# Seven products instead of eight in the down projections of the last two batches

## The chip, the cores and the metric

The kernel runs on one core of a Trainium2 chip. The metric is device time in microseconds, from launch to the end of the last transfer. TensorE (PE) multiplies, VectorE (DVE), ScalarE (ACT) and GpSimd (POOL) work on elements, SyncE (SP) issues most transfers; ACT issues the stores of the output. Each engine works through its own instructions strictly in order.

## The reference

```python
def _attn_ref(q, k, v):                      # 8 batches, 8 heads, 576 positions, 64 wide
    scores = scale * np.matmul(q, k.transpose(0, 1, 3, 2))
    ...
    mask = (rel >= 0) & (rel < window)       # window = 128
    scores = np.where(mask, scores + bias[None], -1000000000.0)
    ...
    return np.matmul(attn, v).astype(np.float32)

def _moe_ref(x, w_a, w_b, w_out):            # 4608 tokens, 512 -> 1536 -> 512
    a = x @ w_a
    b = x @ w_b
    return (a * b @ w_out).astype(np.float32)
```

Windowed attention feeds a feed-forward layer: two up projections, whose results are multiplied element by element, and one down projection by `w_out`. Inputs and result are float32.

## The kernel before

The work goes batch by batch. For batch b TensorE does the **up** projections (hidden values h, 1536 by 576, as 12 blocks f of 128 rows in two halves t of 288 columns) and then the **down** projection (512 by 576, as 4 blocks e of 128 rows and two halves). Float32 accuracy comes from float16 pairs: every operand is kept as a high and a low half, and one product is three matmuls (high·high, high·low, low·high), each 128 by 128 by 288. Six such matmuls are one *step* of the weave below.

In batches 4 to 7 the up projection already uses the scheme of seven products (`up_fast`, lines 926 to 972): a 2 by 2 block product takes seven block products of sums of blocks, instead of eight. The sums of the weights were made earlier (`sums_of_weights`) and lie in the tile `wsum` and in one quarter of `wup`; those of the inputs are made by `split_x` into `xs`. The steps of two blocks f alternate (two lanes), because each block's sums are read from two PSUM banks while the other lane's steps run. `halve` (line 900) makes the float16 pair of a finished block: one cast on ACT, one subtraction on DVE.

The down projection (`down`, line 998) is plain: for each half t and each e it adds 12 blocks times three matmuls in one PSUM bank, ACT scales the bank to `row` (line 1010) and issues its store (line 1011).

Beside batch b's projections runs the attention of batch b+1, as a generator (`attention`, line 712). It works on pairs of heads, numbered i, four to a batch, and yields seven times per pair. `Pace.along` drives it in step with the projections: it names the place of the generator (in pairs) that is to be reached when n steps are done. For one pair the chain is: loads of q and k, squares and scaling, four layout transfers within the core (lines 385 to 388), the score products (`scores`, line 402; tile `sc_ps`), minimum (DVE) and exponential (ACT), `normalize` (line 427: reciprocals, then the probabilities as float16 pairs in `phl`), a transposing transfer `pT<-phl` issued on SP (line 447), the product with v (`pv`, tile `x_ps`), and `keep_x` (line 452: ACT copies the result, squares it; POOL adds the squares to `xq`, line 472). `phl` and `pT` have one buffer each. When a batch's last pair is done, `split_x` makes the operands of its up projection, and `hidden_scale` (line 552, tile `n_ps`) sums the squares on TensorE.

The order of TensorE's instructions from batch 1 on is the order in which the code is written and woven (`manual_schedule` for PE). The order on the other engines, SP among them, is set by a planner ahead of the run, from a model of the durations; `issue_after` sets a floor for some of them. In the last batches before, the attention goes to place 28 beside batch 6's up projection (84 steps), and from 28 to its end at 29 in the first half of the 48 steps of its down projection.

## Time and profile before

| what | value |
|---|---|
| time, three runs | 975.34 us median, 973.39 to 976.2 |
| span of the profiled execution, first to last instruction | 972.1 us |
| time of the profiled execution itself | not on record; the shortest of the three runs is 1.3 us above the span, the median 3.2 us |
| granted TensorE clock | 0.996 |
| TensorE busy | 958.0 us, 99% of the span |
| busy DVE, ACT, POOL | 681.4, 625.8, 260.1 us |
| batch 6's up projection with its attention | 763.8 to 834.4 us |
| batch 6's down projection | 834.4 to 871.5 us |
| batch 7's up and down projection, no attention beside it | 871.5 to 933.6 and to the end |

The times are of whole runs; the span is of one execution that was profiled, and all places below are microseconds from its first instruction. Matmuls are pipelined: a row of the timeline gives the start of its first and the time to the end of its last; the distance between two starts is what a matmul costs.

### The profile page before, as it was taken

The page shows a single profiled execution, that of the slowest core. Times are in us where ns is not written, and L with a number is a line of the kernel's source. Part 1 is how long each engine was busy: PE and PEld are TensorE (multiplying, and loading weights), DVE is VectorE, ACT ScalarE, POOL GpSimd, SP SyncE. Part 2 cuts the span into 40 slices and gives each one's busy share as a digit, 9 for nine tenths or more (in the row PEclk, how much of TensorE's full clock was granted, in tenths as well). Part 3 has the DMA queues.
Part 4 walks back from the last instruction along what each step waited for, and adds up shares of the span by engine and source line. Part 5 has one row for each costly group of instructions (what it writes and reads, how often), then busy time and mean ns, then how long its engine had stood idle before and what let it go on. Part 6 is the DMA issues. An engine that isn't in the chain of part 4 may idle for free.

```text
span 972.1 us, 23845 instructions
## 1 busy us (share of the span) xinstructions
PE 958.0 (99%) x9340; PEld 748.0 (77%) x9341; DVE 681.4 (70%) x1896; ACT 625.8 (64%) x1701; POOL 260.1 (27%) x307
## 2 busy tenths in 40 slices
PE   8989999999999999999999999999999999999998
PEld 6667777777877777777877777777777778777776
DVE  6999997568888668877677867667666676514520
ACT  6877787577767667776766776767666765423321
POOL 1211132045546033531234222401222122301100
PEclk9999999999999999999999999999999999999999
DMA  9473745626437334454336542464245350210001
GB/s 347 143 275 107 260 90 123 161 81 124 90 85 178 69 69 83 100 156 93 65 79 174 103 100 50 112 177 93 45 94 133 117 98 12 57 37 2 1 13 37
DMA packets 148432, 102.82 MB, mean 106 GB/s; under 512 B 120032, under 2 KB 128352, under 8 KB 147296
## 3 DMA queue, kind: packets, MB, share of 16 engines
q1 hardware_dynamic: 138816, 91.77, 38.7%
q10 hardware_dynamic: 9504, 9.54, 3.0%
q8 instruction: 73, 1.20, 0.5%
q14 instruction: 39, 0.32, 0.1%
HBM read 48.33 MB, written 9.44 MB: 59 GB/s over the span
## 4 chain that ended last, share of the span: by engine, by line
PE 89%; DVE 4%; DMA 3%; ACT 3%; issue 1%; SPq 0%; POOL 0%; ACTq 0%; DVEq 0%; POOLq 0%
PE dn_ps L1005 23%; PE ch L909 19%; PE up_ps L909 18%; PE p L909 15%; PE x_ps L543 5%; PE sc_ps L417 4%; PE dn_ps L871 2%; PE sc_ps L413 1%; DMA v<-in_vP 1%; ACT t L626 0%; DMA qst<-qkl 0%; DVE phl L440 0%; DMA qk<-in_kT 0%; DMA qkl<-qkl 0%; PE tr_ps L632 0%
## 5 line engine op out<-in xcount | busy, mean ns | idle before, releaser
L909 PEld LDWEIGHTS <-wup 128*128 128x128 f16 x3072 | 296.5, 98 | 83.8 <-issue 7.4
L1005 PE MATMUL dn_ps<-h,wdn 128*128 128x288 f16 x2016 | 253.9, 286 | 0.0
L1005 PEld LDWEIGHTS <-wdn 128*128 128x128 f16 x2016 | 193.9, 98 | 51.8
L909 PE MATMUL up_ps<-xs,wup 128*128 128x288 f16 x1536 | 196.4, 287 | 2.1 <-DVE v L672 1.1
L909 PEld LDWEIGHTS <-wsum 128*128 128x128 f16 x1152 | 111.7, 98 | 30.9 <-issue 1.3
L964 POOL TENSOR_TENSOR rc<-rc,row 128x288 f32<-128x288 f32 x64 | 61.8, 965 | 275.3 <-DVE row L962 259.4
L423 ACT ACTIVATE t<-t,mn 128x192 f32<-128x192 f32 (+2 forms) x252 | 107.3, 427 | 25.6 <-DVE mn L422 25.3
L440 DVE SCALAR_TENSOR_TENSOR phl<-t,rin,phl 128x192 f16<-128x192 f32 (+2 forms) x252 | 109.6, 476 | 16.9 <-ACT phl L439 16.6
L909 PE MATMUL p<-xs,wup 128*128 128x288 f16 x768 | 115.1, 286 | 0.0
L909 PE MATMUL ch<-xs,wup 128*128 128x288 f16 x768 | 115.1, 286 | 0.0
L909 PE MATMUL ch<-xs,wsum 128*128 128x288 f16 x768 | 111.5, 286 | 0.4 <-ACT rc L934 0.4
L439 ACT ACTIVATE phl<-t,rin 128x192 f16<-128x192 f32 (+2 forms) x252 | 88.9, 426 | 29.7 <-DVE rin L436 15.9
L901 ACT CAST h<-rc 128x576 f16<-128x576 f32 x96 | 64.1, 668 | 63.5 <-DVE rc L969 37.2
L902 DVE TENSOR_TENSOR h<-rc,h 128x576 f16<-128x576 f32 x90 | 69.3, 770 | 30.1 <-ACT h L901 29.3
L422 DVE CUSTOM_DVE_ANT_0 t<-sc_ps,bias,neg 128x192 f32<-128x192 f32 (+2 forms) x216 | 73.6, 388 | 9.9 <-PE sc_ps L417 9.8
L1010 ACT ACTIVATE row<-dn_ps,oi 128x288 f32<-128x288 f32 x56 | 27.6, 494 | 57.5 <-PE dn_ps L1005 57.5
L478 DVE TENSOR_TENSOR xs<-v,xs 128x576 f16<-128x576 f32 x52 | 48.0, 934 | 22.6 <-ACT xs L477 22.5
L946 ACT ACTIVATE row<-ch,g 128x288 f32<-128x288 f32 x64 | 31.8, 497 | 48.9 <-PE ch L909 48.8
L941 DVE TENSOR_TENSOR rc<-p,rc 128x288 f32<-128x288 f32 x64 | 29.0, 454 | 44.6 <-PE p L909 33.8
L398 POOL TENSOR_SCALAR bias<-rel_sb,ninv,sl_sb 128x192 f32<-128x192 f32 x24 | 23.6, 983 | 137.1 <-DVE mn L422 119.1
L909 PE MATMUL p<-xs,wsum 128*128 128x288 f16 x384 | 57.6, 286 | 0.0
L969 DVE SCALAR_TENSOR_TENSOR rc<-rc,g,ch 128x288 f32<-128x288 f32 x64 | 32.6, 510 | 23.6 <-PE ch L909 23.4
(158 smaller groups left out, 1375.8 us busy)
## 6 DMA issues: line engine op xcount, KB each, us to landing
v<-in_vP SPq DMA_DIRECT2D x8, 1280.0 KB, 6.2
out<-row ACTq DMA_DIRECT2D x62, 144.0 KB, 1.9
qk<-in_qT SPq DMA_DIRECT2D x28, 288.0 KB, 4.0
qk<-in_kT SPq DMA_DIRECT2D x28, 288.0 KB, 4.4
wdn<-in_w_a SPq DMA_DIRECT2D x12, 512.0 KB, 5.1
wdn<-in_w_b SPq DMA_DIRECT2D x12, 512.0 KB, 6.1
wdn<-in_w_out SPq DMA_DIRECT2D x12, 512.0 KB, 4.6
qst<-qkh SPq DMA_DIRECT2D x24, 144.0 KB, 2.8
```

What stands on the lines that cost most here:

```text
L417: pe.matmul(ps[64 * e:64 * e + 64, c:c + w], o.qs[:, e, qq], ks[:, e, kk], start=not last, stop=last)
L422: beside[1] = vec.tensor_tensor_reduce(out=t[:, c:c + w], in0=ps[:, c:c + w], in1=o.bias[:, WIN - w:WIN], scale=-0.125 if o.b == 1 else o. ...
L423: beside[0] = act.activation(t[:, c:c + w], t[:, c:c + w], AF.Exp, bias=o.mn[:, n:n + 1], scale=-1.0, accum_out=o.sm[:, n:n + 1])
L439: beside[0] = last_phl[0] = act.activation(phl[:, 0, pc:pc + w], e, AF.Copy, scale=s)
L440: beside[1] = vec.scalar_tensor_tensor(out=phl[:, 1, pc:pc + w], in0=e, scalar=s, in1=phl[:, 0, pc:pc + w], op0=ALU.mult, op1=ALU.subtract)
L478: vec.tensor_tensor(out=xs[:, n, 1, :, :], in0=src, in1=xs[:, n, 0, :, :], op=ALU.subtract)
L543: last = pe.matmul(xp[oc // 512][64 * h:64 * h + 64, o0:o0 + w], vt[0:rows, c:c + 64], probs(pt, rows, blocks, h), start=(n == 0 and first ...
L901: act.copy(h[:, f, :, 0, :], hid)
L902: eng.tensor_tensor(out=h[:, f, :, 1, :], in0=hid, in1=h[:, f, :, 0, :], op=ALU.subtract)
L909: pe.matmul(ps[:, 0:HT], w[:, wi, k, :], xs[:, b, xi, k, :], start=(first and n == 0), stop=(last and n == len(ks) - 1), skip_group_check= ...
L964: pool.tensor_tensor(out=x0, in0=x0, in1=mid, op=ALU.mult)
L1005: pe.matmul(ps[:, 0:HT], wdn[:, f, wi, e * P:(e + 1) * P], h[:, f, t, hi, :], start=(m == 0 and n == 0), stop=(m == NF - 1 and n == 2))
```

## The change

Batches 6 and 7 (`b >= SEVEN`) do their down projection by seven products as well (`down_fast`). The blocks of `w_out`, of the hidden values and of the output are taken as 2 by 2: two blocks f (2j, 2j+1), two halves t, and the output's row blocks e in two groups g, with e and e+2 together. Each group's seven products run over six pairs j with three matmuls: 18 matmuls to a product, 126 to a group, 252 to a batch, where `down` has 288. The two groups alternate product by product.

What this needs:

- Sums of hidden blocks. In these two batches `up_fast` collects two blocks f in a `quad`, `halve_quad` makes four differences per pair on POOL and seven halves instead of four (four casts on ACT, four subtractions on DVE), at set numbers of steps after the pair's last product. Three of the seven have their place in `hx`, in the part of `wup` that belongs to blocks 6 to 11.
- Sums of `w_out` (`sums_of_down`), made once, beside batches 4 and 5: for each of 12 pieces five POOL instructions, a cast, a subtraction, and a transfer of 256 KB to DRAM (`kept_dn`). Three quarters are loaded beside batch 6's up projection into `wdx`, in the part of `wsum` of blocks 6 to 11 (12 transfers of 192 KB); one quarter goes into `wdn` ahead of it (4 transfers).
- Batch 6 works through blocks 6 to 11 first, since their weights are overwritten. Batch 7 needs them again: `keep_up` copies their seven forms to DRAM beforehand (42 transfers of 128 KB), and batch 7's first six blocks load each form into the place of the form just used.
- The attention goes to place 27.2 instead of 28 beside batch 6's up projection. Beside its down projection (42 steps instead of 48) it is paced to reach 30 in 34 steps, so it ends (29) about step 22.

```diff
@@ setup @@
-    xs = const.tile([P, 8, 2, 2, HT], F16, name="xs")
+    xr = const.tile([P, 8 * 4 * HT + 3 * 4 * HT], F16, name="xr")
+    xs = xr[:, 0:8 * 4 * HT].rearrange("p (n w k t) -> p n w k t", n=8, w=2, k=2)
+    hids = cycle([xr[:, (8 + n) * 4 * HT:(9 + n) * 4 * HT]... for n in range(3)])
+    quads = cycle([xr[:, (7 + 2 * n) * 4 * HT:(9 + 2 * n) * 4 * HT]... for n in range(2)])
...
+    def keep_up():
+        for f in range(NF // 2, NF):
+            for n in range(7):
+                sp.dma_start(kept_up[f - NF // 2, :, 4 * P * n:4 * P * n + 4 * P], form_of(f, n))
+                yield
+    def sums_of_down():
...
+            pool.tensor_tensor(out=a[:, 0, :], in0=a[:, 3, :], in1=a[:, 0, :], op=ALU.subtract)
+            pool.tensor_tensor(out=a[:, 2, :], in0=a[:, 2, :], in1=a[:, 0, :], op=ALU.subtract)
+            yield
+            both = work.tile([P, 512], F32, tag="t", name="ws16", bufs=4)...
+            with tc.issue_after(last_main[0].ins):
+                act.copy(both[:, :, 0, :], a)
+            vec.tensor_tensor(out=both[:, :, 1, :], in0=a, in1=both[:, :, 0, :], op=ALU.subtract)
+            sp.dma_start(kept_dn[n], both.rearrange("p a w q -> p (a w q)"))
+            yield
+    def load_down_sums():
+        for n in range(NF):
+            sp.dma_start(wdx[:, n].rearrange("p a w q -> p (a w q)"), kept_dn[n, :, 0:6 * P])
+            yield
...
@@ hidden_scale @@
-            ps = bank("n_ps") if states else ps_at.tile([P, 512], F32, tag="at", name="n_ps")
+            ps = ps_ef.tile([P, 512], F32, tag="ef", name="n_ps") if started["down"] >= SEVEN else bank("n_ps") if states else ...
@@ up_fast @@
+    def halve_slots(h, j, n, x):
+        out = halves_of(h, j, n)
+        act.copy(out[:, :, 0, :], x)
+        vec.tensor_tensor(out=out[:, :, 1, :], in0=x, in1=out[:, :, 0, :], op=ALU.subtract)
+    def difference(out, a, b):
+        pool.tensor_tensor(out=out, in0=a, in1=b, op=ALU.subtract)
+    def halve_quad(h, f, quad, last):
+        j = f // 2
+        b11, b12, b22, b21 = (quad[:, n, :] for n in range(4))
+        if f % 2 == 0:
+            after(1 if last else 2, lambda: halve_slots(h, j, 6, quad[:, 0:1, :]))
+            after(2 if last else 5, lambda: difference(b11, b12, b11))
+            return
+        for n, k, fn in (
+            (2, 1, lambda: halve_slots(h, j, 0, quad[:, 2:4, :])),
+            (3, 1, lambda: difference(b12, b22, b12)),
+            (5, 2, lambda: difference(b22, b22, b11)),
+            (6, 4, lambda: halve_slots(h, j, 2, quad[:, 0:2, :])),
+            (7, 3, lambda: difference(b21, b21, b22)),
+            (10, 5, lambda: halve_slots(h, j, 4, quad[:, 2:4, :])),
+        ):
+            after(k if last else n, fn)
...
+        def load(n):
+            if first_half:
+                sp.dma_start(form_of(where[f], n), kept_up[f, :, 4 * P * n:4 * P * n + 4 * P])
...
         terms(ch, (f, 0), 0, True, True)
+        load(0)
...
+    def down_fast(b, oi, h, pairs):
+        started["down"] = b
...
+        slots = (6, 1, 0, 5, 2, 4, 3)
+        def product(ps, g, q, x, first, last):
+            n = 0
+            for j in pairs:
+                hid = slot_of(h, j, slots[x])
+                for wi, hi in ((0, 0), (0, 1), (1, 0)):
+                    pe.matmul(ps, weight(q, j, wi, g), hid[:, hi, :], start=(first and n == 0), stop=(last and n == 17), skip_group_check=True)
+                    n += 1
+                    if n % 6 == 0 and n < 18:
+                        yield
...
+        def group(g):
+            ch = ps_ch.tile([P, 512], F32, tag="ch", name="dch")[:, 0:HT]
...
+            yield from product(ch, g, 0, 0, True, True)
+            with tc.high_priority(offset=PRIO):
+                last_read[0] = last_main[0] = act.activation(x0, ch, AF.Copy, scale=oi)
+                first_reads[:] = first_reads[1:] + last_read
+            yield
+            ps = ps_ef.tile([P, 512], F32, tag="ef", name="d2")[:, 0:HT]
+            yield from product(ps, g, 1, 1, True, True)
+            with tc.high_priority(offset=PRIO):
+                last_dve[0] = vec.scalar_tensor_tensor(out=x0, in0=ps, scalar=oi, in1=x0, op0=ALU.mult, op1=ALU.add)
+            store(x0, g, 0)
+            yield
...
+        lanes = [group(0), group(1)]
+        for _ in range(7):
+            for lane in lanes:
+                for _ in range(3):
+                    next(lane)
+                    tick()
+                    yield
@@ batch @@
-        weave(att.along(up(states[b], h, plain, fast), n, NPAIR * b + 4), *((spread, *x) for x in quota[b][0]))
-        weave(att.along(down(b, out_scale(states[b]), h, plain + fast), 48, NPAIR * b + 6), *((spread, *x) for x in quota[b][1]))
...
+        for n, z in ((0, 84), (1, 48)):
+            if SEVEN - 2 <= b < SEVEN:
+                sides[n] += [(spread_down, 0, z, 9), (keeping, 0, z, 11)]
+        if b == SEVEN:
+            sides[0] += [(loading, 52, 84, NF)]
+            load_first_sums()
+        weave(att.along(up(states[b], h, plain, fast, seven, b > SEVEN), n_up, NPAIR * b + (3.2 if b == SEVEN else 4)), *sides[0])
+        if seven:
+            weave(att.along(down_fast(b, out_scale(states[b]), h, [f // 2 for f in fast[::2]]), 34, NPAIR * b + 6))
+        else:
+            weave(att.along(down(b, out_scale(states[b]), h, plain + fast), 48, NPAIR * b + 6), *sides[1])
```

How the instructions stand now, at two places. First ACT, around the end of batch 6's up projection: before, from the second half of the last pair's exponentials (line 423) to the last of its probabilities (line 439); the rows between are the up projection's own (PSUM reads of lines 934, 946 and 952, casts of line 901).

```order
L423 ACTIVATE t_12776,sm_12309<-t_12776,mn_12308 128x192 x2
L946 ACTIVATE row_12704<-ch_12702,g_11613 128x288
L952 COPY rc_12703<-p7_12819 128x288
L901 CAST h_774<-rc_12661 128x2x288
L934 COPY rc_12852<-ch_12851 128x288
L901 CAST h_774<-rc_12703 128x2x288
L946 ACTIVATE row_12853<-ch_12851,g_11613 128x288
L435 ACTIVATE rin_12310<-sm_12309 128x4
L952 COPY rc_12852<-p7_12895 128x288
L934 COPY rc_12904<-ch_12903 128x288
L439 ACTIVATE phl_130<-t_12713,rin_12310 128x192 x2
L439 ACTIVATE phl_130<-t_12776,rin_12310 128x192 x2
```

And in the changed kernel, from the first PSUM read of the down projection (line 1180) to the copy of the last pair's product with v (line 504, `keep_x`):

```order
L1180 ACTIVATE row_13017<-dch_13016,oi_13012 128x288
L991 CAST h_778<-xr_125 128x2x288
L471 ACTIVATE t_13108,sm_12533<-t_13108,mn_12532 128x192
L991 CAST wup_120<-xr_125 128x2x288
L1180 ACTIVATE row_13131<-dch_13130,oi_13012 128x288
L483 ACTIVATE rin_12534<-sm_12533 128x4
L487 ACTIVATE phl_134<-t_13045,rin_12534 128x192 x2
L487 ACTIVATE phl_134<-t_13108,rin_12534 128x192 x2
L1172 DMA out_0<-row_13017 128x288
L1172 DMA out_0<-row_13131 128x288
L1191 ACTIVATE xr_125<-dch_13016,oi_13012 128x288
L504 ACTIVATE v_11747<-x_ps_13229 128x512
```

The same piece of attention (old lines 423, 435, 439 are new lines 471, 483, 487) has moved from the up projection into the down projection: its last exponential stands behind the first PSUM read of `down_fast`, its probabilities behind the second. On TensorE 78 matmuls now lie between the pair's last score product and its product with v; before there were 138 of the up projection and 66 of the down projection.

Second SP, at the load of v for batch 5 (during batch 3's down projection); the four layout transfers follow it, for the pair whose scores open batch 4's up projection. Before:

```order
L447 DMA_TRANSPOSE pT<-phl 128x32x128
L297 DMA v<-in_vP 128x2560
L385 DMA qst<-qkh 64x1152
L386 DMA qst<-qkl 64x1152
L345 DMA qk<-in_qT 64x2x576
L387 DMA qkh<-qkh 64x1152
L388 DMA qkl<-qkl 64x1152
```

Now:

```order
L495 DMA_TRANSPOSE pT<-phl 128x32x128
L345 DMA v<-in_vP 128x2560
L296 DMA kept_up<-wup 128x512
L296 DMA kept_up<-wsum 128x512 x3
L433 DMA qst<-qkh 64x1152
L434 DMA qst<-qkl 64x1152
L393 DMA qk<-in_qT 64x2x576
L435 DMA qkh<-qkh 64x1152
L436 DMA qkl<-qkl 64x1152
```

Four copies to DRAM have come between v and the layout transfers. The planner has done the same at the load of v for batch 4; at those for batches 6 and 7 one copy of `kept_dn` stands there.

133 lines of the change are left out of this document (119 added, 14 removed).

## The prediction

> **What bounds the kernel now.** I read the page's busy shares first, then the waits of TensorE, then its timeline around batch 6.
>
> ```profile
> PE 958.0 (99%) x9340; PEld 748.0 (77%) x9341; DVE 681.4 (70%) x1896; ACT 625.8 (64%) x1701; POOL 260.1 (27%) x307
> PE sc_ps L417 <- DMA qkh<-qkh: 1.2, 1, 1.2
> PE sc_ps L417 <- DMA qkl<-qkl: 0.4, 1, 0.4
> 834.42 8.25 PE L1005 MATMUL dn_ps<-h,wdn 128*128 128x288 f16 x66
> 842.59 1.54 PE L543 MATMUL x_ps<-pT,vhl 128*64 128x128 f16 x42
> 844.06 7.52 PE L1005 MATMUL dn_ps<-h,wdn 128*128 128x288 f16 x60
> 851.42 0.41 PE L558 MATMUL n_ps<-xq,ones 128*128 128x512 bf16 x2
> 851.67 20.01 PE L1005 MATMUL dn_ps<-h,wdn 128*128 128x288 f16 x162
> 871.51 0.90 PE L909 MATMUL ch<-xs,wup 128*128 128x288 f16 x6
> ```
>
> TensorE is the bound. In the waits of its engine over the last 430 us I find one place alone, 1.6 us for layout transfers. So a matmul taken away shows in full, as long as no wait takes its place. One costs (871.51 - 851.67) / 162 = 0.1225 us.
>
> **The change part by part. Matmuls.** `down` has 2 x 4 x 12 x 3 = 288 to a batch, `down_fast` 2 x 7 x 6 x 3 = 252, on the same shape (128x288 float16). 72 fewer in two batches, 72 x 0.1225 = **-8.8 us**. The up projections and the attention keep theirs.
>
> **The last pair's product with v.** This is what I expect to give half of it back. The scores of pair 27 (banks 2 and 3) now stand two steps into batch 6's down projection, and only 78 matmuls, 78 x 0.1225 = 9.6 us, lie between them and `x_ps`. In that time the exponentials, `normalize` and the transposing transfer must be through. The rows of the same piece before (ACT, then DVE, SP and the answer on line 447), where the matmul behind the last score started at 817.46:
>
> ```profile
> 817.46 0.91 PE L909 MATMUL p<-xs,wup 128*128 128x288 f16 x6
> 818.55 0.44 ACT L423 ACTIVATE t<-t,mn 128x192 f32<-128x192 f32 x1
> 818.99 0.44 ACT L423 ACTIVATE t<-t,mn 128x192 f32<-128x192 f32 x1
> 827.33 0.20 ACT L435 ACTIVATE rin<-sm 128x4 f32<-128x4 f32 x1
> 828.31 1.49 ACT L439 ACTIVATE phl<-t,rin 128x192 f16<-128x192 f32 x4
> 830.16 0.73 DVE L440 SCALAR_TENSOR_TENSOR phl<-t,rin,phl 128x192 f16<-128x192 f32 x2
> 830.97 4.84 SPq L447 DMA_TRANSPOSE pT<-phl  x1
> DMA to landing us min/median/max: 6.7/7.1/9.2
> ```
>
> Before, the transfer was issued at 830.97, landed some 7 us later, and the product began at 842.59: 4.5 us to spare. Now I count from the matmul behind the last score. The first exponential starts at 818.55 - 817.46 = 1.1 as before. ACT then has, by its order, a PSUM read, a cast, the second exponential, a cast and the second PSUM read ahead of `rin`. For their distances:
>
> ```profile
> 845.19 0.68 ACT L471 ACTIVATE sq<-v 128x576 bf16<-128x576 f32 x1
> 845.78 0.66 ACT L477 CAST xs<-v 128x576 f16<-128x576 f32 x1
> 846.34 0.49 ACT L1010 ACTIVATE row<-dn_ps,oi 128x288 f32<-128x288 f32 x1
> 846.73 0.66 ACT L477 CAST xs<-v 128x576 f16<-128x576 f32 x1
> ```
>
> A cast of 576 columns costs 0.56, a PSUM read 0.39, an exponential 0.44 (818.99 - 818.55). So `rin` starts at 1.1 + 2 x 0.44 + 2 x 0.39 + 2 x 0.56 = 3.9 us; the second PSUM read's matmuls end at 24 x 0.1225 = 2.9 and don't hold it. From `rin` to the last low half of `phl` it took 830.16 + 0.73 - 827.33 = 3.6 us, with two foreign DVE instructions between; now one. I take 2.9, so `phl` is complete at 6.8 and `pT` lands at 6.8 + 7.1 = 13.9. TensorE stands from 9.6 to 13.9: **+4.3 us**. The bounds: `phl` at 6.2 with the shortest landing (6.7) gives 3.3; `phl` at 7.5 with the longest (9.2) gives 7.1. Nothing else in TensorE's order is allowed past `x_ps`, so the whole wait counts. What lies before it (the product with v of pair 26) has its `pT` from far earlier.
>
> **The sums of squares behind it.** `n_ps` needs ACT's copy and square and POOL's addition:
>
> ```profile
> 843.98 0.71 ACT L456 ACTIVATE v<-x_ps 128x512 f32<-128x512 f32 x2 [4.46 <-PE x_ps L543]
> 846.21 1.79 POOL L472 TENSOR_TENSOR xq<-xq,sq 128x576 bf16<-128x576 bf16 x1
> ```
>
> That ends at 848.00, 3.9 us after the last product with v (844.06). Before, 60 matmuls (7.4 us) covered it; now 30 do, 30 x 0.1225 = 3.7 us. The order on ACT and POOL there is the same: **+0.3 us**, bounds 0 and 1.0. After that 132 matmuls (16.2 us) remain until batch 7's first step, so its operands and scale are no issue.
>
> **Transfers on SP's queue.** The 42 copies of up weights and 12 of down sums run beside batches whose TensorE never waits for loads, except at one kind of place: the first scores of batches 3 to 6's up projection, behind v and the layout transfers. Batch 3's and batch 4's, first DMA, then SP and PE:
>
> ```profile
> DMA  9999992667999989995733841799989999787400
> v<-in_vP SPq DMA_DIRECT2D x1, 1280.0 KB, 6.6
> qkl<-qkl SPq DMA_DIRECT2D x1, 144.0 KB, 3.7
> 414.98 0.54 SPq L297 DMA_DIRECT2D v<-in_vP  x1
> 423.53 0.46 SPq L388 DMA_DIRECT2D qkl<-qkl  x1
> 427.79 0.22 PE L417 MATMUL sc_ps<-qkh,qst 128*64 128x64 f16 x2
> 526.80 0.54 SPq L297 DMA_DIRECT2D v<-in_vP  x1
> 533.31 0.47 SPq L385 DMA_DIRECT2D qst<-qkh  x1
> 537.42 0.46 SPq L388 DMA_DIRECT2D qkl<-qkl  x1
> 541.68 0.22 PE L417 MATMUL sc_ps<-qkl,qst 128*64 128x64 f16 x2 [0.42 <-DMA qkl<-qkl]
> ```
>
> The DMA row is the stretch 414 to 429 in 40 slices. At batch 3 the last layout transfer lands at 423.53 + 3.7 = 427.2, 0.6 us before its scores; at batch 4 it is late already. Four copies of 128 KB now stand ahead of the layout transfers: 512 KB at v's rate (1280 KB in 6.6 us) are 2.6 us of queue. Around v's end (414.98 + 6.6 = 421.6) the engines idled for about 1.6 us, by the digits 57338417 (4.2 of 8 slices of 0.375 us); the copies fill that first. So 2.6 - 1.6 - 0.6 = 0.4 us at batch 3; at batch 4, with v issued 533.31 - 526.80 = 6.5 us ahead of the layout transfers, I take 0; at batches 5 and 6 (256 KB, 1.3 us) 0. Together **+0.5 us**; the upper bound, with nothing absorbed, is 2.0 + 2.6 + 1.3 + 1.3 = 7.2. The other copies stand in batch 0 and where SP idles. Each of batch 7's 42 loads is issued 42 steps (31 us) before its use.
>
> **More work on ACT, DVE and POOL.** In batch 6's up projection six pairs add three half-size casts and subtractions each and four differences on POOL:
>
> ```profile
> 763.80:834.40 70.60, 70.60 (x709) 55.56 (x707) 47.75 (x132) 45.64 (x124) 15.76 (x15) 1.00 0.27 52
> L902 DVE TENSOR_TENSOR h<-rc,h 128x576 f16<-128x576 f32 x11 | 8.5, 772 | 3.5 <-ACT h L901 3.4
> L440 DVE SCALAR_TENSOR_TENSOR phl<-t,rin,phl 128x192 f16<-128x192 f32 (+2 forms) x18 | 6.8, 417 | 0.0
> L422 DVE CUSTOM_DVE_ANT_0 t<-sc_ps,bias,neg 128x192 f32<-128x192 f32 (+2 forms) x18 | 6.1, 391 | 3.0 <-PE sc_ps L417 3.0
> L964 POOL TENSOR_TENSOR rc<-rc,row 128x288 f32<-128x288 f32 x11 | 10.8, 982 | 48.3 <-DVE row L962 44.8 <-ACT rc L934 3.4
> L478 DVE TENSOR_TENSOR xs<-v,xs x7: 742/760/1829, 831.2 to 852.8; 128x576 f16<-128x576 f32 x7
> ```
>
> The first row is that stage (length; PE, PEld, DVE, ACT, POOL busy). DVE gains 9 x 0.77 = 7 (four subtractions for two, one of them of half size) and loses 0.8 of a pair's attention, 0.8 x (6.8 + 6.1) / 2 = 5; it stays near 50 us. POOL gains 24 x 0.98 = 24 and comes to 39. The stage is 84 x 6 x 0.1225 = 61.7 us of projection and 70.6 - 61.7 = 8.9 of two pairs' attention, so with 1.2 pairs 67. The two engines also hold each other up: the last row has the same subtraction at 0.74 and, beside a busy POOL, at 1.83 us. If POOL fills 39 / 67 = 0.6 of the stage, 24 subtractions lose 24 x 0.6 x half of 1.09 = 8 us, and DVE comes to 58 of 67. I cost this at **0**: TensorE is covered by the other lane's steps. If that cover goes, a pair's halves are late for the pair after next, which writes in the same quad (the second rival). In batches 4 and 5 each stage gets three of the twelve pieces of `w_out`'s sums; batches 1 to 3 carried 24 pieces of the same five POOL instructions, and TensorE's list has no wait above 0.5 us there: 0.
>
> [...]
>
> **Sum**: -8.8 + 4.3 + 0.3 + 0.5 = **-3.7 us** on the span of 972.1. The time of that execution is not on record; the median of the runs is 3.2 us above its span. I put the same difference on the median: 975.34 - 3.7 = **971.6**. Own range, with the wait from 3.3 to about 6: 969.8 to 973.6.
>
> **The rivals.** *The wait is hidden*: `pT` lands by 9.6, and the whole 8.8 us show, 966.5. Against it: `phl` and 6.7 us of landing alone exceed 9.6 unless `phl` is done at 2.9, before ACT reaches `rin`. *POOL and DVE hold up the pairs*: with DVE at 58 us of 67 a halving comes late; the four pairs of batch 6 that start in a used quad each lose 1 us, -3.7 + 4 = +0.3, 975.6. For it: the subtractions and POOL's differences meet in every pair. Against it: 10 steps (7.4 us) are set for a pair's tail. *SP's queue decides, and the kernel is slower*: the copies ahead of the layout transfers hold up four up projections for the full 7.2 us, -8.8 + 4.6 + 7.2 = +3.0, 978.3. It decides from where the added queue exceeds idle time and spare, 2.2 us at batch 3, and nothing at batch 4 if its idle time is used up by late copies. For it: TensorE's only late wait is there. *Not done as said*: the order of instructions shows the 72 matmuls gone; 975.3.
>
> **How the numbers follow.** Chances: forecast 0.66, hidden 0.06, POOL and DVE 0.15, SP's queue 0.11, not done 0.02. About 0.3% (2.9 us) is what a measurement can tell from no change, and the forecast's range straddles it: of its 0.66 I give 0.43 to faster than 972.4. With the hidden case 0.49 faster; the rest of the forecast, POOL and DVE, and not done make 0.38 same; SP's queue and the upper end of the others 0.13 slower. The range reaches from 968.8 (the smallest wait, 969.8, and a us of scatter of the median) to 976.2 (past the second rival).
>
> **What would show it.** Right: a wait of TensorE at the last `x_ps` on DMA pT, 3 to 6 us long, the only new one over 1 us; the last `phl` about 7 us behind the last score. Wrong: no wait there, then the gain is 8 to 9 us; waits of `sc_ps` on `qkh` or `qkl` above 1.6 us in all, then SP's queue; waits of `ch` steps on ACT in batch 6, then POOL and DVE. The sum fails also if a matmul of the seven products costs more than 0.1225.

## The result, and the profile after

The changed kernel took 985.81 us (median; 984.04 to 986.96), the kernel before beside it 975.03: a ratio of 1.0116, 95% interval 1.0099 to 1.0133. It is slower by 1.2%, where I had forecast 971.6 and a range up to 976.2. The profiled span grew from 972.1 to 983.4 us, by 11.3, where my sum gave -3.7. So some 15 us of cost are missing in it. Two of the twelve executions of the run "POOL, batch 7" below took 997 us, at a granted clock of 0.945 and 0.947 where its others had 0.996 or 0.998, and are left out of its median.

The page of the changed kernel, busy time and instructions of each engine:

```profile
PE 953.5 (97%) x9268; PEld 742.3 (75%) x9269; DVE 725.6 (74%) x1944; ACT 641.9 (65%) x1737; POOL 340.7 (35%) x415
```

The 72 matmuls are gone, and TensorE stands for 30 us in place of 14. Its waits over the whole span, largest first, those of the start of the program and two others, of 0.8 and 0.4 us, left out (engine, tile, what it waited for; us in total, times, longest):

```profile
PE x_ps L591 <- DMA pT<-phl: 4.7, 1, 4.7
PE ch L958 <- DVE xr L1080: 3.5, 4, 1.2
PE sc_ps L465 <- DVE mn L470: 2.9, 4, 1.7
...
PE ch L958 <- DVE xr L1094: 2.0, 3, 0.8
PE ch L958 <- ACT xr L1053: 1.7, 4, 0.7
PE sc_ps L465 <- DMA qkh<-qkh: 1.0, 1, 1.0
...
PE sc_ps L465 <- DMA qkl<-qkl: 0.4, 1, 0.4
```

The wait that I forecast is the first row. The waits for transfers (`qkh`, `qkl`) were there before, 1.6 us in all. The other new ones, from `ch` to `sc_ps`, are readings of banks by DVE and ACT, which I had costed at nothing. Where they lie is told by stage. The rows are batch 4's up projection, batch 5's, batch 6's, batch 6's down projection, batch 7's up, batch 7's down (start and end; length; busy PE, PEld, DVE, ACT, POOL; granted clock; share and rate of DMA). First the kernel before:

```profile
538.99:611.60 72.61, 71.04 (x710) 55.68 (x708) 52.74 (x150) 50.78 (x135) 17.66 (x20) 1.00 0.41 83
652.32:723.10 70.78, 70.78 (x711) 55.58 (x709) 50.24 (x142) 48.80 (x129) 16.32 (x16) 1.00 0.35 74
763.81:834.42 70.61, 70.61 (x710) 55.56 (x708) 47.77 (x132) 45.66 (x124) 15.76 (x15) 1.00 0.27 52
834.42:871.51 37.09, 37.09 (x334) 29.65 (x332) 10.53 (x18) 8.62 (x17) 7.53 (x5) 1.00 0.17 45
871.51:933.39 61.88, 61.88 (x507) 49.30 (x505) 30.20 (x58) 22.40 (x48) 8.73 (x11) 1.00 0.01 4
933.39:968.54 35.15, 35.15 (x289) 28.08 (x287) 1.62 (x4) 4.18 (x8) 0.79 (x1) 1.00 0.09 30
```

And the changed kernel:

```profile
540.14:616.22 76.08, 71.68 (x710) 55.74 (x708) 59.44 (x154) 53.42 (x141) 29.08 (x36) 1.00 0.43 97
656.94:730.55 73.61, 71.27 (x711) 55.65 (x708) 57.61 (x149) 52.37 (x137) 27.68 (x34) 1.00 0.40 90
771.26:842.54 71.28, 68.73 (x651) 53.65 (x649) 52.78 (x130) 45.51 (x119) 30.68 (x36) 1.00 0.40 95
842.54:886.43 43.89, 37.49 (x356) 29.50 (x354) 20.43 (x44) 15.46 (x39) 11.72 (x10) 0.92 0.21 49
886.43:949.01 62.58, 62.04 (x506) 49.30 (x504) 35.14 (x68) 26.07 (x58) 25.48 (x33) 1.00 0.31 91
949.01:979.76 30.75, 30.75 (x253) 24.56 (x251) 6.34 (x10) 5.31 (x10) 2.90 (x4) 1.00 0.10 35
```

The differences are +3.5, +2.8, +0.7, +6.8, +0.7 and -4.4 us; batch 4 begins 1.15 us later, and 0.1 lies behind the last matmul: 11.3 together. The down projections of batches 4 and 5 take 40.7 us in both kernels.

Two of these rows need one correction. Some 58 matmuls of attention moved from batch 6's up projection to its down projection (710 records to 651; 334 to 356 with 36 fewer of its own). They are 42 products with v (1.51 us in the timeline) and 16 score products (0.35 us for eight), with the changes between tiles about 2.3 us by my estimate. So batch 6's up projection lost about 0.7 + 2.3 = 3.0 us, and its down projection lost about 6.8 + 4.4 - 2.3 = 8.9.

**Batch 6's down projection.** Its timeline around the last product with v (start, duration, engine, instruction; in brackets the idle time before it and what ended it):

```profile
847.63 0.27 PE L465 MATMUL sc_ps<-qkh,qst 128*64 128x192 f16 x2 [1.66 <-DVE mn L470]
...
854.48 0.74 DVE L488 SCALAR_TENSOR_TENSOR phl<-t,rin,phl 128x192 f16<-128x192 f32 x2
855.29 5.36 SPq L495 DMA_TRANSPOSE pT<-phl  x1
862.54 2.77 PE L591 MATMUL x_ps<-pT,vhl 128*64 128x128 f16 x42 [4.72 <-DMA pT<-phl]
865.25 3.29 PE L1166 MATMUL dch<-wup,wsum 128*128 128x288 f16 x18
```

The wait is 4.72 us. But the 42 products with v then took 2.71 us to the next start, not 1.47 as before, and the 18 matmuls behind them 3.12 (to 868.37), not 2.2: 2.2 us more. The same stretch cut into windows, TensorE alone (length, busy PE, granted clock, DMA):

```profile
857.82:860.30 2.48, 0.00 (x0) 1.00 1.09 214
860.30:862.54 2.24, 0.00 (x0) 0.50 0.88 171
862.54:867.14 4.60, 4.60 (x51) 0.50 0.00 0
867.14:870.00 2.86, 2.86 (x24) 1.00 0.02 6
```

2.5 us into the wait the granted clock fell to 0.50, and it stayed there until 867.14. That is where the 2.2 us went. So the wait cost 4.7 + 2.2, and the scores of the first timeline row another 1.7: 8.5 of the 8.9 us.

**Batches 4 and 5.** The end of batch 5's up projection; batch 4's looks the same, 114 us earlier:

```profile
727.63 1.77 DVE L317 TENSOR_TENSOR ws<-xr,ws 128x512 f16<-128x512 f32 x1
729.32 0.45 DVE L1080 TENSOR_TENSOR xr<-ch,xr 128x288 f32<-128x288 f32 x1
727.43 1.41 POOL L539 TENSOR_TENSOR v<-v 128x576 f32<-128x576 f32 x1
729.82 0.90 PE L958 MATMUL ch<-xr,wsum 128*128 128x288 f16 x6 [1.19 <-DVE xr L1080]
```

Line 317 is the subtraction that makes the low half of a piece of `w_out`'s sums. It stands in DVE's queue ahead of the reading of `ch` on line 1080. Ten of the twelve take 0.67 to 0.69 us; this one and batch 4's, each beside a POOL instruction, took 1.77 and 1.76. TensorE may not add to that `ch` bank before the reading, and waits. TensorE's idle time grew by 2.8 us in batch 4 (76.08 - 71.68 for 72.61 - 71.04) and by 2.3 in batch 5 (73.61 - 71.27, none before). The rest is busy time with no more matmuls, 0.64 us for four further waits and 0.49 for three, so some 0.16 us go with each wait.

**Batch 6's first steps** are held by the sums too:

```profile
774.13 0.40 ACT L1053 COPY xr<-ch 128x288 f32<-128x288 f32 x1 [0.81 <-DVE ws L317]
774.58 0.90 PE L958 MATMUL ch<-xr,wsum 128*128 128x288 f16 x6 [0.69 <-ACT xr L1053]
```

The first quad of hidden rows lies where the sums are computed (the eighth place of the inputs), so its first copy waits for the last piece, and TensorE stands for 0.7 us.

### The profile page after: what moved, and what is told of

Its sections match the earlier page's. It is cut to its first block, busy times and chain, and to the rows that moved or that the text cites. A ratio compares the mean times of both kernels' runs of the same rounds, so it can differ in the third digit from the quotient of the medians.

```text
span 983.4 us, 24091 instructions
## 1 busy us (share of the span) xinstructions
PE 953.5 (97%) x9268; PEld 742.3 (75%) x9269; DVE 725.6 (74%) x1944; ACT 641.9 (65%) x1737; POOL 340.7 (35%) x415
## 4 chain that ended last, share of the span: by engine, by line
PE 67%; DVE 15%; ACT 6%; DMA 6%; issue 3%; POOL 1%; SPq 1%; ACTq 0%; DVEq 0%; POOLq 0%
PE ch L958 18%; PE p L958 13%; PE dn_ps L1141 13%; PE up_ps L958 11%; PE x_ps L591 3%; PE sc_ps L465 3%; PE dch L1166 3%; DVE phl L488 3%; PE d L1166 3%; DMA v<-in_vP 2%; DMA pT<-phl 2%; DVE wsum L147 1%; DVE wsum L149 1%; DVE t L470 1%; ACT t L471 1%
## 5 line engine op out<-in xcount | busy, mean ns | idle before, releaser
L958 PE MATMUL up_ps<-xr,wup 128*128 128x288 f16 x1536 | 196.7, 287 | 2.8 <-DVE v L720 2.0
L1141 PE MATMUL dn_ps<-h,wdn 128*128 128x288 f16 x1440 | 182.6, 286 | 0.0
L1141 PEld LDWEIGHTS <-wdn 128*128 128x128 f16 x1440 | 137.7, 98 | 37.5
L1088 POOL TENSOR_TENSOR xr<-xr,row 128x288 f32<-128x288 f32 x64 | 61.8, 966 | 168.2 <-DVE row L1086 153.3
L958 PE MATMUL ch<-xr,wup 128*128 128x288 f16 x768 | 115.0, 286 | 2.5 <-DVE xr L1094 2.0
L958 PE MATMUL ch<-xr,wsum 128*128 128x288 f16 x768 | 111.2, 286 | 5.2 <-DVE xr L1080 3.5
L958 PE MATMUL p<-xr,wup 128*128 128x288 f16 x768 | 115.1, 286 | 0.0
L470 DVE CUSTOM_DVE_ANT_0 t<-sc_ps,bias,neg 128x192 f32<-128x192 f32 (+2 forms) x216 | 73.7, 388 | 5.3 <-PE sc_ps L465 5.1
L526 DVE TENSOR_TENSOR xr<-v,xr 128x576 f16<-128x576 f32 x52 | 48.3, 941 | 25.5 <-ACT xr L525 25.5
L950 DVE TENSOR_TENSOR h<-xr,h 128x576 f16<-128x576 f32 x66 | 51.3, 778 | 19.1 <-ACT h L949 18.6
L958 PE MATMUL p<-xr,wsum 128*128 128x288 f16 x384 | 57.5, 286 | 0.0
L1061 DVE TENSOR_TENSOR xr<-p,xr 128x288 f32<-128x288 f32 x64 | 29.1, 454 | 30.7 <-PE p L958 25.3
```

The lines of the kernel that those rows point to most:

```text
L470: beside[1] = vec.tensor_tensor_reduce(out=t[:, c:c + w], in0=ps[:, c:c + w], in1=o.bias[:, WIN - w:WIN], scale=-0.125 if o.b == 1 else o. ...
L526: vec.tensor_tensor(out=xs[:, n, 1, :, :], in0=src, in1=xs[:, n, 0, :, :], op=ALU.subtract)
L950: eng.tensor_tensor(out=h[:, f, :, 1, :], in0=hid, in1=h[:, f, :, 0, :], op=ALU.subtract)
L958: pe.matmul(ps[:, 0:HT], w[:, wi, k, :], xs[:, b, xi, k, :], start=(first and n == 0), stop=(last and n == len(ks) - 1), skip_group_check= ...
L1088: pool.tensor_tensor(out=x0, in0=x0, in1=mid, op=ALU.mult)
L1141: pe.matmul(ps[:, 0:HT], wdn[:, f, wi, e * P:(e + 1) * P], h[:, f, t, hi, :], start=(m == 0 and n == 0), stop=(m == NF - 1 and n == 2))
```

## The experiments

All are edits of the changed kernel unless said otherwise. The table has the length of each stage, from first to first matmul of the projections, in us, and the time. A stage's length comes from one profiled execution. Six runs share the changed kernel's code in the up projections of batches 4 and 5 (the change, later product, filled wait, free bank, no differences, two halvings); there they took 75.7 to 77.1 and 73.6 to 74.2 us, so smaller differences than these say nothing there. The four of them that also share batch 6's took 71.3 to 71.4.

| run | up 4 | down 4 | up 5 | down 5 | up 6 | down 6 | time | ratio to before |
|---|---|---|---|---|---|---|---|---|
| before | 72.6 | 40.7 | 70.8 | 40.7 | 70.6 | 37.1 | 975.0 | |
| the change | 76.1 | 40.7 | 73.6 | 40.7 | 71.3 | 43.9 | 985.8 | 1.0116 |
| later product | 75.8 | 40.7 | 73.6 | 40.7 | 71.3 | 41.8 | 984.2 | 1.0096 |
| filled wait | 75.7 | 40.7 | 73.7 | 40.7 | 71.4 | 42.8 | 984.3 | 1.0102 |
| free bank | 76.1 | 40.7 | 74.1 | 40.7 | 71.3 | 36.7 | 977.9 | 1.0037 |
| no differences | 77.1 | 40.7 | 74.2 | 40.7 | 71.1 | 43.0 | 985.3 | 1.0107 |
| two halvings | 76.1 | 40.7 | 74.1 | 40.7 | 70.0 | 46.2 | 986.8 | 1.0128 |
| sums in down | 74.4 | 41.5 | 74.8 | 40.9 | 80.0 | 49.8 | 999.8 | 1.0248 |
| sums on POOL | 73.9 | 40.7 | 72.8 | 40.7 | 71.8 | 43.9 | 984.0 | 1.0104 |
| batch 7 only | 72.6 | 40.7 | 73.4 | 40.7 | 71.8 | 38.0 | 977.1 | 1.0023 |
| sums spread | 77.6 | 40.7 | 72.3 | 40.7 | 72.4 | 36.7 | 983.0 | 1.0089 |
| scores apart | 76.0 | 40.7 | 72.4 | 40.7 | 73.1 | 36.1 | 980.3 | 1.0059 |
| copies held | 77.8 | 40.7 | 79.1 | 40.7 | 73.2 | 36.2 | 987.0 | 1.0123 |
| sums early | 70.9 | 41.9 | 73.9 | 41.6 | 73.8 | 36.1 | 985.9 | 1.0117 |
| batch 7, early | 72.3 | 41.7 | 77.9 | 41.5 | 76.2 | 37.1 | 983.6 | 1.0098 |
| sums all POOL | 74.7 | 40.7 | 73.2 | 40.7 | 71.6 | 36.7 | 977.2 | 1.0025 |
| POOL, batch 7 | 72.5 | 40.7 | 72.5 | 40.7 | 72.9 | 38.9 | 977.2 | 1.0026 |
| POOL and scores | 75.2 | 40.7 | 73.3 | 40.7 | 72.3 | 36.1 | 976.5 | 1.0021 |

### The wait and the clock

**Later product.**

```diff
-            weave(att.along(down_fast(...), 34, NPAIR * b + 6))
+            weave(att.along(down_fast(...), 52, NPAIR * b + 6))
```

> The attention beside batch 6's down projection is spread over 52 steps' pace in place of 34, so that 114 matmuls (14.0 us) and not 78 (9.6 us) stand between the last scores and the last product with v; all else is the changed kernel's. In its trace that product began 14.5 us behind the last scores, after a wait of 4.7, and the granted clock was 0.50 for the 4.6 us behind it. Theory A, the wait and the halved clock belong together: wait 0.5 us or none, clock 1.00 throughout, the stage 43.9 - 4.2 - 2.3 = 37.4 us, about 979.3 in all. Theory B, the clock falls for another reason: wait 0.5, still some 4.6 us at 0.50, stage 39.7, about 981.6. Theory C, the sums of squares or batch 7's operands, now 4.4 us later, become a wait of their own: stage or start of batch 7's up projection 2 us or more longer than in A.

Measured: the wait at the product with v is gone and the clock holds through it (0.96 over the stage, the loss of it in the windows below), but the stage is 41.8, not 37.4. A new wait stands in front of the second sums of squares. From the waits of that run:

```profile
PE n_ps L606 <- DVE xtop L607: 3.2, 1, 3.2
```

And windows over the place, columns as above:

```profile
872.15:875.40 3.25, 0.01 (x2) 0.00 (x0) 3.05 (x4) 0.78 (x2) 0.89 (x1) 1.00 0.12 41
875.40:878.85 3.45, 3.45 (x16) 2.21 (x16) 1.61 (x7) 0.00 (x0) 0.00 (x0) 0.51 0.02 6
```

Theory C, with A's clock: 3.25 us without work, and behind them 3.45 us at 0.51.

**Filled wait.**

```diff
+            if b == SEVEN:
+                for _ in product(ps, g, 1, 1, True, True):
+                    pass
             yield from product(ps, g, 1, 1, True, True)
```

> The changed kernel with 36 matmuls done twice in batch 6's down projection (the second product's, both halves, started over, so that the result is the same), just ahead of the last product with v: 4.4 us of work where TensorE stood for 4.7. Theory A, the clock is halved because TensorE stands: the product with v begins at the same place, with a wait of 0.3, the clock stays 1.00, the stage takes 43.9 - 2.3 = 41.6 us, 983.5 in all. Theory B, the clock falls for another reason: stage 43.9, 4.6 us at 0.50, 985.8. Theory C, the product with v is late for a reason that goes with TensorE's place and not with the transposing transfer: the 4.4 us come on top, stage 46 or more.

Batch 6's down projection as a window of that run:

```profile
842.31:885.06 42.75, 39.91 (x392) 31.57 (x390) 20.45 (x44) 15.35 (x39) 11.70 (x10) 1.00 0.22 50
```

The product with v starts where it did, with 36 useless matmuls in place of the wait, and the clock stays at 1.00: theory A. The stage is 1.1 us shorter and not 2.3: 0.4 us of the wait are left, and the next taker of a bank now waits 0.7 us for the maximum of the sums of squares, at a clock of 1.00.

**Free bank.**

```diff
-            ps = ps_ef.tile(..., tag="ef", name="n_ps") if started["down"] >= SEVEN else ...
+            ps = ps_at.tile(..., tag="at", name="n_ps") if started["down"] >= SEVEN else ...
```

(with the 52 steps)

> As the run with the later product (the attention beside batch 6's down projection at 52 steps' pace), and the two banks of the sums of squares are taken from attention's three banks in place of the three that the seven products' second banks use. There the wait of 4.7 us at the product with v had gone, and the second sums of squares waited 3.2 us for a bank, with the clock at 0.50 for 3.4 us behind it. Theory A, it waited because the two halves' products held the other two banks: no wait above 0.5 us there, clock 1.00 throughout, the stage 41.8 - 3.2 - 1.7 = 36.9 us, about 979.5 in all. Theory B, the sums of squares are late because DVE reaches the maxima late, whatever the bank: the wait stays or moves to the next taker of a bank of attention, stage above 40.

```profile
844.06:880.75 36.69, 35.11 (x357) 28.10 (x354) 20.04 (x44) 15.55 (x39) 12.15 (x10) 1.00 0.24 54
```

Theory A, and 7.2 us less than in the changed kernel (43.89): the two edits take back all of the wait and the clock. The 1.6 us at the last scores are still in it. The time is 977.9, still slower than before (interval 1.0023 to 1.0051).

### Batch 6's up projection

**No differences.**

```diff
     def difference(out, a, b):
+        if started["down"] >= SEVEN - 1:
+            return
```

> The four differences on POOL of each pair of columns in batches 6 and 7 are left out, so the sums of the hidden rows are not computed; casts, subtractions and matmuls stay. In the changed kernel batch 6's up projection takes 71.3 us, with four waits of 0.4 to 0.8 us and 3.4 us of gaps in all, where its matmuls and its share of attention need 67. Theory A, POOL's instructions hold up DVE's: the gaps go, the stage takes 67 to 68, about 982 in all. Theory B, ACT and DVE have too many instructions of their own between the steps: the stage stays at 71 within 0.5, about 985.8. Between the two: the share that goes is POOL's.

**Two halvings.**

```diff
-            after(1 if last else 2, lambda: halve_slots(h, j, 6, ...))
+            if started["down"] >= SEVEN: after(...)
...
-            after(k if last else n, fn)
+            if n < 10 or started["down"] >= SEVEN: after(...)
```

> In batch 6's up projection alone two of the four halvings of each pair of columns are left out (the third full one and the half-size one: 12 casts on ACT, 12 subtractions on DVE), so that two products of its down projection read old data. ACT's and DVE's casts and subtractions are then as many as in the kernel before; POOL's differences, the places of the rest and the share of attention stay the changed kernel's. Its stage took 71.3 us, its own work and attention being 68.2. Theory A, the number of instructions on ACT and DVE costs the 3 us: stage 68.5 to 69.2. Theory B, the order in which the rest falls (a run of the softmax's subtractions, the first step behind the last sums of w_out) costs them: stage 70.5 to 71.3.

Batch 6's up projection in the one and in the other:

```profile
773.25:844.35 71.10, 68.93 (x652) 53.65 (x649) 51.46 (x130) 46.14 (x121) 14.04 (x16) 1.00 0.41 96
772.48:842.44 69.96, 68.73 (x651) 53.64 (x649) 49.12 (x121) 41.80 (x112) 30.94 (x37) 1.00 0.41 97
```

POOL's time halved (30.7 to 14.0 us) and the stage stayed: in this stage POOL's differences are not what costs. With 12 casts and 12 subtractions fewer the stage is 1.3 us shorter. Two of its four larger gaps went, the first (the sums' leftover, 0.7) and one behind ACT (0.4) stayed. So the number of instructions on ACT and DVE accounts for 1.3 of 3.0 us, and the sums' last piece for 0.7. Why ACT's reading is 0.4 us late stays open. The remaining 0.6 is hardly idle time, since the four gaps together are 2.5 us; it is busy time, or an error of the 2.3 us taken above for the moved matmuls.

The same two runs tell what the wait ahead of the last scores is, 1.66 us at the start of the changed kernel's down projection. First without the differences, then with two halvings:

```profile
848.16 0.27 PE L465 MATMUL sc_ps<-qkh,qst 128*64 128x192 f16 x2 [0.38 <-DVE mn L470]
846.14 0.27 PE L465 MATMUL sc_ps<-qkh,qst 128*64 128x192 f16 x2 [0.27 <-DVE mn L470]
```

Leaving out either takes most of it away. In the changed kernel DVE has five of the softmax's low halves (line 488) ahead of the reading, 1.64 us for two and 1.60 for three; without POOL's differences they take 1.07 and 1.06.

### The sums of w_out

**Sums in down.**

```diff
-                sides[n] += [(spread_down, 0, z, 9), (keeping, 0, z, 11)]
+                sides[n] += [(keeping, 0, z, 11)] + ([(spread_down, 0, z, 18)] if n else [])
```

> The twelve pieces of w_out's sums (POOL's five instructions, ACT's cast, DVE's subtraction, the copy out) stand beside the down projections of batches 4 and 5 alone, six to each, and no longer beside their up projections; all else is the changed kernel's. In its trace the up projections of batches 4 and 5 take 76.1 and 73.6 us (72.6 and 70.8 in the kernel before), their down projections 40.7 as before. Theory A, the pieces beside the steps of seven products hold up DVE and with it TensorE: 72.6 and 70.8 again, downs 40.7, 6.3 us saved, about 979.5 in all. Theory B, the copies of up weights on SP's queue do it, which stay where they were: 76.1 and 73.6, about 985.8. Theory C, the loss moves along with the pieces: ups 72.6 and 70.8, downs near 44, about 985.8.

Neither theory. Batch 4's up projection, now without pieces, lost the three gaps on DVE (it has none above 0.3 us behind its first 10 us), which speaks for A. Its 74.4 us, 1.8 more than before, hold 3.4 us at a clock of 0.50 (last section); its matmuls are busy for 1.7 us longer (72.71 for 71.04). But pieces were left over and ran on into batch 6, in ACT's order ahead of the first readings. From ACT's timeline:

```profile
777.96 0.62 ACT L316 CAST ws<-xr 128x512 f16<-128x512 f32 x1 [2.45 <-POOL xr L312]
```

ACT stood in its queue at the cast for POOL's sum, and all readings of banks behind it stood too; TensorE's longest wait for one was 4.3 us.

**Sums on POOL** (the low halves).

```diff
-            vec.tensor_tensor(out=both[:, :, 1, :], in0=a, in1=both[:, :, 0, :], op=ALU.subtract)
+            pool.tensor_tensor(out=both[:, :, 1, :], in0=a, in1=both[:, :, 0, :], op=ALU.subtract)
```

> The changed kernel with the low halves of w_out's sums (one subtraction of 512 columns to a piece, 0.67 to 1.77 us) on POOL in place of DVE; places and all else unchanged. In the changed kernel's up projections of batches 4 and 5 TensorE loses 0.6 to 1.4 us at three places in each where this subtraction, or an instruction of DVE beside it, stands ahead of a reading of a bank. Theory A, the subtraction's place on DVE is the cost: the stages go from 76.1 and 73.6 to about 72.9 and 71.1 us, 980 in all. [...]

2.2 and 0.8 us less, where A wanted 3.2 and 2.5. The gaps behind line 317 went; in batch 5 one of 0.7 us came, on ACT's reading of a bank, and in both stages the scores' wait for DVE stayed, at 0.7 us.

**Batch 7 only.**

```diff
-SEVEN = 6
+SEVEN = 7
```

> Seven products in batch 7's down projection alone; batch 6 is as in the kernel before (last pairs of attention beside its up projection), nothing is loaded back but the sums of w_out, which are now made in batches 5 and 6. Against the kernel before's stages: batch 7's down projection 30.75 in place of 35.16 (-4.4), its up projection +0.7, batch 6's down projection 37.1 with no wait at the product with v and no halved clock, batch 4 as before. Theory A, the sums cost some 3 us in each up projection beside which they are made, whatever batch it is: batches 5 and 6 at 73.6 and 73.5, 975.1 - 4.4 + 0.7 + 1.1 + 5.8 = 978.3 in all. Theory B, the sums cost little where batch 4's first scores are not late as well: batches 5 and 6 near 71, 973 in all.

Between the two: the sums cost batch 5 2.6 us and batch 6 1.2 in the up projection and 0.9 in the down, and batch 7's up projection took 63.4 us for 61.9. Batch 7's down projection takes 30.75 us again. Batch 4 is as before, with all 42 copies of up weights still issued, so the copies are not what lengthened it in the changed kernel. With half of the gain the time is 977.1 (1.0014 to 1.0032).

**Sums spread** (with the free bank).

```diff
+        if SEVEN - 3 <= b < SEVEN:
+            sides[1] += [(spread_down, 0, 40, 12)]
```

> As the run with the free bank (977.9), and w_out's sums are made beside the down projections of batches 3, 4 and 5, four pieces to each and done by their fortieth step, none beside an up projection. The run that put six to a down projection had shown that a piece takes POOL 8 to 9 us and that what is left over stalls ACT in the next up projection; four fit. Theory A, the pieces beside the up projections' seven products are the cost, and beside plain products they are hidden: up projections of batches 4, 5 and 6 at 72.6, 70.8 and 70.4 us in place of 76.1, 74.1 and 71.3, down projections at 40.7, about 970.2 in all. Theory B, the pieces cost the same wherever they stand: the down projections of batches 3 to 5 grow by 2 us each, about 976. Theory C, the up projections of batches 4 and 5 are late by the copies of up weights: 76 and 74 stay, 977.

Batch 5 went from 74.1 to 72.3, but batch 4 from 76.1 to 77.6. The last piece of each down projection ran over its end. Two waits and the clock make most of batch 4's loss: 1.5 us for a layout transfer and 2.4 for a reading, and a granted clock of 0.96 over the stage, with 73.28 us of busy time where the changed kernel has 71.68. ACT and TensorE at batch 4's third step, from the timeline:

```profile
549.55 0.62 ACT L316 CAST ws<-xr 128x512 f16<-128x512 f32 x1 [2.45 <-POOL xr L312]
...
551.52 0.88 PE L958 MATMUL ch<-xr,wsum 128*128 128x288 f16 x3 [2.42 <-ACT xr L1053]
```

**Sums early** (with the scores apart, below).

```diff
-            sides[1] += [(spread_down, 0, 40, 12)]
+            sides[1] += [(spread_down, 0, 24, 12)]
```

> As the run with the scores apart (980.3), but each four pieces of w_out's sums are asked for within the first 24 steps of the down projections of batches 3 to 5 and not within 40. In that run the last piece of each ran on into the up projection behind it, ACT's cast stood in its queue for POOL's sum, and the readings of banks behind it were late (2.5 us at batch 4's third step). Theory A, that tail is what is left of the sums' cost: up projections of batches 4, 5 and 6 from 76.0, 72.4 and 73.1 to 72.6, 70.8 and 70.4 us, down projections at 40.7, 980.3 - 7.7 = 972.6 in all or less. Theory B, pieces closer together stall ACT inside the down projections in place of it: these grow, and the time stays at 978 or more.

Theory B. Batch 4's up projection has no gap left, and the loss stands one stage earlier, in batch 3's down projection (47.0 us for 41.4 with the scores apart), where TensorE waits 3.3 us for DVE's scale and the granted clock is 0.96 over the stage. The window of batch 4's up projection, and the wait in batch 3:

```profile
545.74:616.66 70.92, 70.92 (x710) 55.57 (x708) 52.93 (x148) 50.26 (x135) 21.06 (x25) 1.00 0.39 85
```

```profile
PE qtot L415 <- DVE oi L1229: 3.3, 1, 3.3
```

**Batch 7, early.** Batch 7 only, without `keeping`, the pieces in `(spread_down, 0, 24, 12)` beside the down projections of batches 4 to 6.

> Seven products in batch 7's down projection alone, the sums of w_out made in the first 24 steps of the down projections of batches 4 to 6, and no copies of up weights, which nothing needs then. Theory A (the sums cost nothing beside plain products when done early; the copies in the first batch cost about 1 us): batch 4 begins at 539.0 to 539.5, up projections of batches 4, 5 and 6 at 72.6, 70.8 and 70.6, down projections 40.7, 40.7 and 37.1, batch 7's 62.6 and 30.75: the time of before, 974.3, less 4.4 and plus 0.7 = 970.6. Theory B, the sums cost where they stand: some 2 us in each of three down projections, 976; batch 4's beginning at 540 or later would tell that the copies are not what delays it.

Theory B: attention's chain came late instead, and the first scores of batch 5 waited for it (4.2 us, one wait, on ACT's exponential). Batch 4 began at 540.9 without any copy of up weights.

**Sums all on POOL** (with the free bank).

```diff
-            with tc.issue_after(last_main[0].ins):
-                act.copy(both[:, :, 0, :], a)
-            vec.tensor_tensor(...)
+            pool.tensor_copy(both[:, :, 0, :], a)
+            pool.tensor_tensor(...)
```

(and 36 steps in place of 48 in batch 5's down projection)

> As the run with the free bank (977.9), with both halves of w_out's sums made by POOL (its own cast and subtraction), at the changed kernel's places except that the last three pieces are asked for in 36 of batch 5's 48 steps, so that they are through before batch 6. Neither ACT nor DVE has an instruction of the sums any more. Theory A, what costs is an instruction of the sums in ACT's or DVE's queue, ahead of a reading of a bank: up projections of batches 4, 5 and 6 from 76.1, 74.1 and 71.3 to 72.9, 71.1 and 70.5 us, down projections at 40.7, 977.9 - 7 = 971 in all. Theory B, POOL's instructions themselves hold up DVE, and there are 28 us more of them: up projections of batches 4 and 5 stay at 74 or above, 976 or more.

In between: batches 4 and 5 at 74.7 and 73.2. No instruction of the sums stands in ACT's or DVE's queue, yet 1.2 us are lost at one place in each. Batch 4's:

```profile
569.49 1.27 POOL L316 TENSOR_TENSOR ws<-xr,ws 128x512 f16<-128x512 f32 x1
569.66 1.71 DVE L949 TENSOR_TENSOR h<-xr,h 128x576 f16<-128x576 f32 x1
571.29 0.50 DVE L1093 SCALAR_TENSOR_TENSOR xr<-xr,g,ch 128x288 f32<-128x288 f32 x1
571.84 0.90 PE L957 MATMUL ch<-xr,wup 128*128 128x288 f16 x6 [1.23 <-DVE xr L1093]
```

A halving's subtraction, 0.75 us on average in the kernel before (line 902), took 1.71 beside POOL's new subtraction, 1.0 us more, and the reading of `ch` behind it was late.

**POOL, batch 7** and **POOL and scores**: the same, with `SEVEN = 7` and no copies, and with the step ahead of the last scores.

> Seven products in batch 7 alone (977.05 in the run of that name), the sums of w_out made wholly by POOL beside batches 5 and 6, and no copies of up weights. Theory A: batch 5's up projection from 73.4 to 71.1, batch 6's from 71.8 to 70.7, its down projection from 38.0 to 37.1, batch 7's 62.9 and 30.75: 977.05 - 4.3 = 972.8 in all, and batch 4 begins at 539.0 to 539.5 if the copies were what delayed the first batch. Theory B, POOL's longer work holds up DVE: the stages stay within 0.5, 976.5.

> As the run with the sums all on POOL, and the last pair's last scores a step later with attention at 54 steps' pace, which took batch 6's down projection from 36.7 to 36.1 where it was tried. Expected 0.6 us below that run: 970.4 by theory A there, 975.4 or more by theory B.

977.2 and 976.5 (1.0011 to 1.0031): by the time, theory B in both. In the first, batch 5 gained 1.0 us against "batch 7 only" and batch 6 lost 1.1 and 0.9. The second is the best version with seven products in both batches. None of the kernels beat the kernel before.

### The last scores and the copies

**Scores apart** (with the sums spread).

```diff
+            if i == n - 1:
+                yield i + 3.3 / 7
             if two == 2 and p in (1, 3):
```

(54 steps)

> As the run before it in this row (sums beside the down projections of batches 3 to 5), and one step of six matmuls stands ahead of the last pair's last scores, which in all kernels so far waited 1.6 to 1.7 us there for DVE to read a bank; the attention's pace goes from 52 to 54 steps to keep 114 matmuls ahead of the last product with v. Theory A, the bank is read in time, 0.74 us of the wait are covered by the step and the rest goes partly with it: the stage 36.7 - 1 = 35.7, 969 in all. Theory B, DVE is late by its own queue (the softmax's subtractions of pair 26 and a halving) and a step earlier or later changes nothing: 36.7.

36.7 to 36.1 us; the wait went from 1.6 to 0.8. A, at half its size.

**Copies held** (with the scores apart; `last_sp` is the transposing transfer issued last).

```diff
+                with tc.issue_after(last_sp[0].ins):
+                    sp.dma_start(kept_up[...], form_of(f, n))
```

> As the run with the scores apart, and the 42 copies of up weights are held behind the transposing transfer that was issued last where the program asks for them, so that 18 of them no longer stand among the first batch's loads; all now run in batches 4 and 5. Theory A, these 18 cost the first batch the 0.5 to 1.5 us by which the changed kernels reach batch 4 later than the kernel before (539.7 to 541.3 against 539.0): batch 4 begins at 539.0 to 539.5, some 968 in all. Theory B, that is scatter: no change there. Theory C, on SP's queue ahead of the layout transfers they hold up the first scores of batches 4 to 6: waits of scores on transfers grow from 1 us to 2 or more, 970 or later.

Theory C. Batch 4 begins at 541.5, as in the run with the scores apart (541.4), and the scores' waits on the layout transfers, 2.8 us in that run (1.4 in the changed kernel), are now 6.6 + 2.2:

```profile
PE sc_ps L466 <- DMA qkh<-qkh: 6.6, 2, 5.2
```

## Why the prediction was wrong, point by point

By its own steps, on the span: -8.8 (matmuls), +4.7 (the wait), +2.2 (the clock behind it), +1.7 (the last scores), +3.5 and +2.8 (batches 4 and 5), +3.0 (batch 6's up projection), +0.7 (batch 7's), +1.2 (before batch 4) and +0.1 make +11.1 of the 11.3 measured.

- **Matmuls, -8.8: right.** Batch 7's down projection went from 35.15 to 30.75 us, 36 matmuls of 0.122. Every variant has the 30.75.
- **The last product with v, +4.3: right in mechanism and size, 4.72.** `phl` was complete 7.1 us behind the last scores (I had 6.8), the transfer landed 7.25 later (7.1).
- **What the wait does to TensorE: not in the sum, +2.2.** I let the wait end with the transfer, and the prediction has no term for the clock. The traces show a clock of 0.50 from 2.5 us into the wait of 4.72 until 867.14, and the filled wait, with work in place of the wait and a clock of 1.00 over the stage, shows that standing is the cause.
- **The sums of squares, +0.3: no wait in the changed kernel.** The step looked at ACT and POOL alone. The bank was the closer limit: moved later, the same sums waited 3.2 us for one.
- **SP's queue, +0.5: about 0.** The scores' waits on transfers are 1.4 us, 1.6 before. The planner had put 18 copies into the first batch. Held behind, they took the scores' waits from 2.8 to 8.8 us: the rival was real, its condition not met.
- **More work on ACT, DVE and POOL, "I cost this at 0": the step that failed.** It is 3.5 + 2.8 + 3.0 us, and the 1.7 of the scores belong to it (their wait is 0.4 or 0.3 us when POOL's differences or two of the halvings are left out): 11.0 of the 15 us that the sum lacked. Two sentences of it were wrong. "TensorE is covered by the other lane's steps": the lanes have one `ch` bank each, which is read and added to again; a reading late by more than the other lane's one or two steps holds TensorE. And the comparison with batches 1 to 3, which carried 24 such pieces without waits: there, by the quotas in `batch`, the pieces stand beside down projections and plain up steps, not beside steps of seven products; in the trace before, all but the last of the 24 start there. A busy share of 58 us in 67 (52.8 in 71.3 measured) said that DVE has room; what counts is whether one foreign instruction of 0.7 us, or of 1.7 beside POOL, comes just ahead of a reading.
- **The rival "POOL and DVE hold up the pairs"** named this mechanism, but in batch 6 alone and with 4 us. In batch 6's up projection the loss is 3.0, of which POOL's differences make some 0.2 (71.3 to 71.1) and the added halvings on DVE and ACT 1.3; what POOL does to DVE shows at the last scores (five low halves in 1.64 and 1.60 us, without POOL's differences in 1.07 and 1.06). The larger part of the loss lies where I had excluded it.
- **Batch 7's loads, 0: no wait for them.** Its +0.7 is for the most part one wait, 0.5 us, for a reading of `ch` at the end of the up projection, behind two halvings.
- **Open:** why batch 4 begins 1.2 us later. It began between 539.4 and 543.8 in the twelve variants with no sums beside batch 3, at 540.0 and 540.9 in the two of them without copies, and at 538.99 in the one profile of before; the copies are not shown to be the cause. The four executions of the kernel before are themselves 2.8 us apart (973.39 to 976.2), so this may be scatter. The last 1.0 us of batch 6's up projection is in part open too.

Was there a place for the sums without cost? Six placings were tried, and each time part of the loss stayed or came up elsewhere: DVE's queue, ACT's queue behind POOL, a subtraction of DVE's beside POOL's (1.71 us for 0.75), the start of the next stage, the attention's chain. That these three engines have no free place of this size beside steps of seven products is my reading of the six, not shown for every placing.
